# Two value loads cast on the way, key sums as products of their own, the ninth query chunk apart, W2 in five parts: a fused attention and feed-forward kernel on one core

## The chip, the core and the metric

The kernel runs on one core of one Trainium2 chip. The metric is device microseconds for one execution; lower is better. TensorE (PE), VectorE (DVE), ScalarE (ACT), GpSimd (POOL) and SyncE (SP) run side by side and wait for each other by semaphores. SP and GpSimd each issue DMA transfers on a queue of their own; in the profile SP's is the hardware queue q1 and GpSimd's the software queue q0.

## The reference

```
q_s = softmax of q over its 64 columns          # q, k, v: 8 batches x 8 heads x 576 x 64
k_s = softmax of k over the 576 rows
kv  = einsum('bhsd,bhse->bhde', k_s, v)         # 64 x 64 for each head
x   = einsum('bhsd,bhde->bhse', q_s, kv)        # laid out as 4608 tokens x 512
h   = x @ w_in                                  # 512 x 2048
g   = where(h > 0, h, exp(min(h, 0)) - 1)
out = g @ w_out                                 # 2048 x 512
```

## The kernel before, in words

The attention is done in sixteen **units**, each half the heads of one batch: unit n belongs to batch n // 2. A unit has 576 rows, cut into 9 **chunks** of 64. The feed-forward part works on nine **blocks** of 512 tokens. Block 0 takes the first 8 chunks of batch 0, which are units 0 and 1; the ninth chunk of each belongs to block 1.

For a unit, ACT takes the exponential of q (tile `QR`) and of k (`KR`, written as bfloat16 into the tile's own first half). DVE sums the rows of q (`ZQ`) and takes reciprocals (`RZQ`); DVE and POOL multiply (`QS`, float16). PE turns `QS` through the identity matrix `ID`, and a copy brings the result from PSUM (`PS`) to `qsT`. The value tile `VR` is cast to bfloat16 in `VB`, whose 65th column holds ones, so that one set of 36 small products (`kv_mm`, 64x65 each) gives the key-value matrix in 64 columns and the key sums in the 65th. `m` takes the reciprocals of those sums (`RZK`) and writes the scaled matrix to `MBLK`. A product of `MBLK` and `qsT` (`ao_parts`, `ao_mm`) gives x, which is copied to `XT`.

For a block, `hg_mm` multiplies `XT` by `W1` in eight groups of two tiles; `hg` applies the activation on ACT and DVE into `GR`; `out_mm` multiplies `GR` by `W2`. From block 2 on the second product is done in seven instead of eight quarter products (`pair`, L806). In block 0 the first three groups go part by part over the four slices kc of `W1`: slices 0 and 1 need `XT` of unit 0, slices 2 and 3 that of unit 1.

Even units use the buffers numbered 0 and odd units those numbered 1. Before the first product of block 0, PE multiplies the identity by itself (L892) where the plan sees it idle.

The order of the instructions on each engine is written out in the table `ORDER`: operations are numbered as the program creates them, and each engine's row lists the numbers. So a wait holds up everything behind it on its engine. Semaphore waits come from the tiles that each operation reads and writes.

At the start SP loads q of units 0 and 1, k and v of unit 0, k and v of unit 1, 576 KB each. GpSimd's queue loads the weights, and its first weight load waits for k of unit 0 (`gate`). Units 2 and 3 and `W2` (four parts of 1 MB) follow on GpSimd's queue.

Of the kernel before, what the change touches and what calls it, by code (L numbers as in the profile page):

```python
# [17 lines left out]
CH = 9  # L18
# [31 lines left out]
    "act": (  # L50
# [12 lines left out]
    "dve": (  # L63
# [37 lines left out]
}  # L101

AFTER = ((208, 196), (227, 255), (234, 268), (300, 281))


class Op:
    __slots__ = ("eng", "dur", "emit", "deps", "key", "idx", "start", "end",
                 "dma", "sem", "val", "clock", "nbytes", "side", "early", "alts")

# [157 lines left out]
def t_dve(n, fast=1):  # L267
    return n / 0.96 / fast + 74


def t_f32r(n):
    return (n + 32) / 2.4

# [816 lines left out]
```

## Time and profile before

| | |
|---|---|
| median of 3 runs | 292.26 us (292.03 to 292.69) |
| span of the profiled execution | 290.4 us, first to last instruction |
| median less span | 1.9 us; the page gives no total of its own for the profiled execution, so a span is turned into a time by adding this |
| PE busy | 280.6 us of the span (97%) |
| DVE, ACT, POOL busy | 225.5, 209.7, 167.8 us |
| first product of block 0 starts | 14.20 us |
| last product ends | 287.06 us |
| DMA | 36.70 MB read, 9.44 MB written |

The page gives busy times and shares, 40 slices of the span, the chain of work that ended last, and the costliest groups. A row of the timeline is: start, duration, engine, line, operation, tile written and read, count, and in brackets the idle time before it and what ended it. L277 is a copy helper, so its rows are told apart by their tiles.

### The profile page before, as it was taken

The numbers are of one execution on the slowest core, as the hardware profiler recorded it, in microseconds if no ns is written. First come the engines' busy times: TensorE is split into PE (matmuls) and PEld (weight loads), VectorE is DVE, ScalarE is ACT, GpSimd is POOL, SyncE is SP. The second block draws the span as 40 slices with busy tenths as digits, with TensorE's granted clock in tenths as the row PEclk, the third lists the DMA queues.
The fourth block names the chain that finished last, engine by engine and source line by source line (L and its number), as shares of the span: only waits on it lengthen the run. The fifth ranks groups of instructions, "written<-read, shape, count | busy, mean of one in ns | idle before, by whom it ended". The sixth has DMA issues, their size and how long they took to land.

```text
span 290.4 us, 5465 instructions
## 1 busy us (share of the span) xinstructions
PE 280.6 (97%) x2176; PEld 243.7 (84%) x2176; DVE 225.5 (78%) x425; ACT 209.7 (72%) x237; POOL 167.8 (58%) x161
## 2 busy tenths in 40 slices
PE   2899999999999999999999999999999999999995
PEld 0488787778888899989999988989999999988995
DVE  3758834777699978989996987688977786794884
ACT  4857839989899899968995598975385656665510
POOL 1991335523869778676574886757314234277741
PEclk9999999999999999999999999999999999999999
DMA  7999999798896838739939295313102002300334
GB/s 259 399 363 390 389 389 339 163 260 323 238 349 163 241 91 228 202 78 305 178 96 222 56 292 129 76 40 71 46 18 56 0 2 67 78 2 1 92 73 128
DMA packets 36474, 50.04 MB, mean 172 GB/s; under 512 B 16352, under 2 KB 18144, under 8 KB 36448
## 3 DMA queue, kind: packets, MB, share of 16 engines
q1 hardware_dynamic: 29680, 33.96, 43.7%
q0 software_dynamic: 6528, 15.47, 17.8%
q8 instruction: 17, 0.28, 0.5%
q10 hardware_dynamic: 240, 0.26, 0.3%
q14 instruction: 9, 0.07, 0.1%
HBM read 36.70 MB, written 9.44 MB: 159 GB/s over the span
## 4 chain that ended last, share of the span: by engine, by line
PE 94%; DMA 2%; POOL 2%; SPq 0%; issue 0%; DVE 0%
PE PS L620 46%; PE PS L806 32%; PE PS L673 10%; PE PS L538 3%; DMA KR<-in_k_dram 2%; PE PS L507 2%; POOL W L377 1%; POOL VB L277 0%; PE PS L457 0%; POOL QS L433 0%; SPq L359 0%; PE PS L550 0%; DVE OSB L815 0%
## 5 line engine op out<-in xcount | busy, mean ns | idle before, releaser
L620 PE MATMUL PS<-XT,W 128*128 128x512 f32 x576 | 142.0, 393 | 0.1
L620 PEld LDWEIGHTS PS<-XT,W 128*128 128x128 f32 x576 | 105.0, 188 | 21.2 <-DVE GR L659 0.5
L652 DVE SCALAR_TENSOR_TENSOR GR<-PS,GE 128x512 fp32r<-128x512 f32 x112 | 76.8, 686 | 18.7 <-ACT GE L648 16.7
L646 ACT ACTIVATE GE<-PS 128x1024 f32<-128x1024 f32 x56 | 57.4, 1025 | 40.0 <-PE PS L620 34.2
L757 POOL TENSOR_TENSOR GR<-GR 128x256 fp32r<-128x256 f32 (+1 forms) x48 | 47.2, 996 | 31.5 <-DVE SB L757 16.6
L648 ACT ACTIVATE GE<-GE 128x1024 f32<-128x1024 f32 x56 | 59.4, 1061 | 1.4
L806 PE MATMUL PS<-W,GR 128*128 128x256 f32 x336 | 53.7, 283 | 0.0
L806 PE MATMUL PS<-TB,GR 128*128 128x256 f32 x336 | 51.3, 283 | 0.0
L806 PEld LDWEIGHTS PS<-W,GR 128*128 128x128 f32 x336 | 47.6, 191 | 1.7
L806 PEld LDWEIGHTS PS<-TB,GR 128*128 128x128 f32 x336 | 45.7, 191 | 0.7
L433 POOL TENSOR_TENSOR QS<-QR,RZQ 128x1152 f16<-128x1152 f32 (+1 forms) x16 | 30.4, 1898 | 21.4 <-DVE RZQ L423 19.7
L815 DVE TENSOR_TENSOR OSB<-OSB,PS 128x256 f32<-128x256 f32 x84 | 34.7, 416 | 10.3 <-PE PS L806 9.2
L673 PE MATMUL PS<-W,GR 128*128 128x512 f32 x128 | 32.7, 396 | 0.0
L757 POOL TENSOR_TENSOR GR<-SB,GR 128x256 fp32r<-128x256 f32 (+1 forms) x18 | 17.3, 971 | 24.6 <-PE PS L806 12.7
L673 PEld LDWEIGHTS PS<-W,GR 128*128 128x128 f32 x128 | 23.3, 188 | 5.0 <-DMA W<-in_moe_w_out_dram 0.5
L757 POOL TENSOR_TENSOR SB<-GR 128x256 fp32r<-128x256 f32 (+1 forms) x20 | 19.2, 965 | 13.7 <-DVE GR L652 6.4
L421 DVE TENSOR_REDUCE ZQ<-QR 128x18 f32<-128x1152 f32 (+2 forms) x18 | 21.7, 1207 | 6.1 <-ACT QR L419 4.8
L757 DVE TENSOR_TENSOR GR<-GR 128x256 fp32r<-128x256 f32 (+1 forms) x36 | 21.3, 603 | 0.6 <-PE PS L806 0.6
L277 POOL CAST VB<-VR 128x1152 bf16<-128x1152 f32 (+1 forms) x11 | 11.9, 1084 | 13.1 <-DMA VR<-in_v_dram 13.1
L646 ACT ACTIVATE ESB<-PS 128x1024 f32<-128x1024 f32 x16 | 16.1, 1024 | 4.5 <-PE PS L620 3.4
L399 ACT ACTIVATE KR<-KR 128x1152 bf16<-128x1152 f32 x16 | 18.4, 1155 | 0.8 <-DMA KR<-in_k_dram 0.8
L277 ACT ACTIVATE XT<-PS 128x512 fp32r<-128x512 f32 (+6 forms) x23 | 13.6, 595 | 6.3 <-PE PS L538 3.2
(58 smaller groups left out, 271.4 us busy)
## 6 DMA issues: line engine op xcount, KB each, us to landing
out_dram<-OSB SPq DMA_DIRECT2D x61, 128.0 KB, 2.4
QR<-in_q_dram SPq DMA_DIRECT2D x12, 576.0 KB, 4.9
KR<-in_k_dram SPq DMA_DIRECT2D x12, 576.0 KB, 6.3
VR<-in_v_dram SPq DMA_DIRECT2D x12, 576.0 KB, 5.1
W<-in_moe_w_out_dram POOLq DMA_DIRECT2D x4, 1024.0 KB, 16.7
QR<-in_q_dram POOLq DMA_DIRECT2D x4, 576.0 KB, 12.1
VR<-in_v_dram POOLq DMA_DIRECT2D x4, 576.0 KB, 13.0
KR<-in_k_dram POOLq DMA_DIRECT2D x4, 576.0 KB, 11.1
```

The lines of the kernel that those rows point to most:

```text
L277: return e.activation(dst, src, AF.Copy) if e is self.nc.scalar else e.tensor_copy(dst, src)
L399: S.add("act", t_act(1152, False), lambda e: e.activation(ek[:, :, :, :].rearrange("p h c d -> p (h c d)"), flat(k), AF.Exp), key - 2, X=[ ...
L421: S.add("dve", t_dve(m), lambda e, qp=qp, zp=zp: e.tensor_reduce(zp, qp, AX.X, ALU.add), key - 3, R=[f"qR{i}{x}" for x in xs], W=[f"ZQ{i}{ ...
L433: lambda e, qp=q[:, :, a:b, :], rz=rz, dst=qs[:, :, a:b, :]: e.tensor_tensor(dst, qp, rz, ALU.mult),
L620: last = e.matmul(P[:, t * 512:(t + 1) * 512], self.W1[:, kc, tt * 128:(tt + 1) * 128], self.XT[:, kc, rc:rc + BLK], start=(kc == 0), stop ...
L646: S.add("act", t_act(1024, True), lambda e: e.activation(ge, P, AF.Exp), key, W=own, X=banks)
L648: S.add("act", t_act(1024, False), lambda e: e.activation(ge, ge, AF.Relu, bias=1.0, scale=-1.0), key, X=own)
L652: S.add("dve", t_dve(512 if j else 1024), lambda e, u=u: e.scalar_tensor_tensor(*(x[:, :, u, :] if j else x for x in (gt, P)), 0.0, ge[:, ...
L673: last = e.matmul(dst, self.tile(jb, jj, ts), self.W2[:, jj, c0:c1], start=(jj == 0), stop=(jj == 15))
L757: lambda e: e.tensor_tensor(dst, a, b, op), key, R=R, W=W, X=X, after=after)
L806: last = e.matmul(dst, a[i][:, y_, :], b[i][:, y_, :], start=start and i == 0 and y_ == 0, stop=stop and i == len(grps) - 1 and y_ == z - ...
L815: S.add("dve", t_dve(256), lambda e: e.tensor_tensor(dst, a, b, ALU.add), key, R=R, W=W, X=X, after=after)
```

## The change

- `load`: v of units 0 and 1 is loaded as bfloat16, into the first half of its own raw tile (`vp`). The casts to `VB` of these two units go. The two loads move from SP's queue to GpSimd's, and k of unit 1 with them. SP now issues three loads at the start: q of units 0 and 1, k of unit 0. v of unit 0 waits, in GpSimd's row, for q of unit 0 to land; the old `gate` of the first weight load goes.
- `key_sums`, `kv_plain`: for units 0 and 1 the 65th column is a set of 36 products of its own (64x1) with its own reciprocal, ahead of the 36 products of k and v (64x64).
- `stage_q`, `parts`, `rest`: the ninth query chunk of units 0 and 1 is staged, turned and multiplied apart, during block 0. Units 2 and 3 are cut into 7 and 2 chunks, and so are their loads of q.
- `load_w2`: `W2` comes in parts of 4, 4, 4, 2 and 2 tiles of 16; k and v of unit 3 stand ahead of the last two. The first product's last quarter in block 0 is cut in two accordingly.
- The exponentials of block 0 go to `GE` rather than to two `ESB` buffers; four `ESB` buffers serve the first half of block 1.
- `ORDER` is written anew for all engines.

The core of the diff:

```diff
-    def load(self, n, t, key, eng="gp"):
+    def load(self, n, t, key, eng="gp", c0=0, c1=CH, after=()):
...
+        if t == "v" and n in self.PLAIN:
+            dst = self.vp(n)[:, :, :, :].rearrange("p h c d -> p h (c d)")
...
+    PLAIN = (0, 1)
...
+    def key_sums(self, n, ps, key):
...
+                        last = e.matmul(P[hs, x:x + 1], ek[fs, h, c, :], VB[fs, h, c, D:D + 1],
+                                        start=(c == 0), stop=(c == CH - 1))
+            return last
+        S.add("pe", 400, mm, key, R=[f"kR{i}", f"VBone{vb}"], X=banks, side=1)
...
+        S.add("dve", 82, lambda e: e.reciprocal(rz[:, :].unsqueeze(2), PZ), key,
+              W=[f"RZK{i}"], X=banks)
...
+    def kv_plain(self, n, ps):
...
+                        last = e.matmul(P[hs, x:x + D], ek[fs, h, c, :], v[fs, h, c, :],
+                                        start=(c == 0), stop=(c == CH - 1))
...
-        for n, t in ((0, "q"), (1, "q"), (0, "k"), (0, "v"), (1, "k"), (1, "v")):
+        for n, t in ((0, "q"), (1, "q"), (0, "k")):
             self.load(n, t, -40, "sp")
-            if (n, t) == (0, "k"):
-                gate = S.ops[-1]
-        self.load_w1(0, 3, (0,), -30, [gate])
+        self.load(0, "v", -40, after=S.ops[-3:-2])
+        self.load(1, "k", -40)
+        self.load_w1(0, 3, (0,), -30)
+        self.load(1, "v", -40)
...
-        for g0, g1 in ((3, 4), (4, 5), (5, 6), (6, 8)):
+        for g0, g1 in ((3, 4), (4, 6), (6, 8)):
...
-        self.stage1(0, -8, vconv=CAST0)
+        self.stage1(0, -8)
         self.tp(0, AB, -9, TP0)
-        self.side(C, -6, self.kv_mm(0, C))
-        self.stage1(1, -5, vconv=CAST1)
+        self.key_sums(0, C, -7)
+        self.side(C, -6, self.kv_plain(0, C))
+        self.stage1(1, -5)
...
-        self.load(2, "q", -28)
-        self.load_w2(0, -29)
-        self.load_w2(1, -29)
-        for n, t in ((2, "k"), (2, "v"), (3, "q")):
+        self.load(2, "q", -28, c1=7)
+        self.load_w2(0, 4, -29)
+        self.load_w2(4, 8, -29)
+        for n, t in ((2, "k"), (2, "v")):
             self.load(n, t, -28)
-        self.load_w2(2, -27)
-        self.load_w2(3, -25)
+        self.load(3, "q", -28, c1=7)
+        self.load_w2(8, 12, -27)
         for t in "kv":
             self.load(3, t, -26)
+        for jj in (12, 14):
+            self.load_w2(jj, jj + 2, -25)
...
     "sp": (
-        "8 9 10 11 12 13 204 206 183 180 187 189 186 209 228 190 218 219 235 229 301 302 184 238 "
+        "8 9 10 230 232 209 206 213 215 212 235 254 216 244 245 261 255 327 328 210 264 375 207 "
```

How the table moves the instructions is seen in three places at the start. On ACT, before, from the first exponential of q to the copy of x (the brackets name the semaphores waited for: `D_` a load, by tile and issuing queue, `S_` an engine):

```order
L419 ACTIVATE QR0<-QR0 128x2x256 [waits D_qR0sp]
L419 ACTIVATE QR0<-QR0 128x2x320
L419 ACTIVATE QR1<-QR1 128x2x320 [waits D_qR1sp]
L399 ACTIVATE KR0<-KR0 128x1152 [waits D_kR0sp]
L277 ACTIVATE qsT0<-PS3 128x512 [waits S_pe]
L277 ACTIVATE VB0<-VR0 128x2x5x64 [waits D_vR0sp]
L419 ACTIVATE QR1<-QR1 128x2x256
L277 ACTIVATE qsT1_55<-PS1 128x640 [waits S_pe]
L277 ACTIVATE qsT0<-PS3 128x640 [waits S_pe]
L399 ACTIVATE KR1<-KR1 128x1152 [waits D_kR1sp]
L277 ACTIVATE VB1<-VR1_56 128x2x5x64 [waits D_vR1sp]
L277 ACTIVATE XT<-PS2 128x512 [waits S_pe]
```

The same stretch of ACT now:

```order
L431 ACTIVATE QR0<-QR0 128x2x256 [waits D_qR0sp0]
L431 ACTIVATE QR0<-QR0 128x2x256
L431 ACTIVATE QR1<-QR1 128x2x256 [waits D_qR1sp0]
L431 ACTIVATE QR1<-QR1 128x2x256
L412 ACTIVATE KR1<-KR1 128x1152 [waits D_kR1gp0]
L431 ACTIVATE QR0<-QR0 128x2x64
L412 ACTIVATE KR0<-KR0 128x1152 [waits D_kR0sp0]
L431 ACTIVATE QR1<-QR1 128x2x64
L282 ACTIVATE qsT0<-PS3 128x512 [waits S_pe]
L282 ACTIVATE qsT0<-PS3 128x512
L282 ACTIVATE XT<-PS2 128x512 [waits S_pe] x2
```

The two casts are gone, and the exponential of unit 1's keys, loaded by GpSimd's queue, now stands ahead of that of unit 0's keys, loaded by SP; both copies of unit 0's x are ACT's.

On POOL, before, from the first scaling of q to the second cast:

```order
L433 TENSOR_TENSOR QS0<-QR0,RZQ0 128x2x4x64 [waits S_dve]
L377 DMA W1<-in_moe_w_in_dram 128x1x768 [waits D_kR0sp]
L377 DMA W1<-in_moe_w_in_dram 128x1x768
L277 CAST VB0<-VR0 128x2x4x64 [waits D_vR0sp]
L377 DMA W1<-in_moe_w_in_dram 128x1x768 x2
L377 DMA W1<-in_moe_w_in_dram 128x4x256
L433 TENSOR_TENSOR QS1_54<-QR1,RZQ1 128x2x4x64 [waits S_dve]
L277 CAST VB1<-VR1_56 128x2x4x64 [waits D_vR1sp]
```

The same stretch of POOL now, from the identity matrix on:

```order
L343 AFFINE_SELECT ID<-ID 128x128
L367 DMA KR1<-in_k_dram 128x2x576
L367 DMA VR0<-in_v_dram 128x2x576 [waits D_qR0sp0]
L390 DMA W1<-in_moe_w_in_dram 128x1x768
L367 DMA VR1_56<-in_v_dram 128x2x576
L444 TENSOR_TENSOR QS0<-QR0,RZQ0 128x2x4x64 [waits S_dve]
L390 DMA W1<-in_moe_w_in_dram 128x1x768 x2
L444 TENSOR_TENSOR QS1_54<-QR1,RZQ1 128x2x4x64 [waits S_dve]
L367 DMA QR0<-in_q_dram 128x2x448 [waits S_gp]
L390 DMA W1<-in_moe_w_in_dram 128x1x768
```

Three loads of units 0 and 1 now stand on this engine, the first slice of `W1` between the two value loads, and 7 chunks of unit 2's q ahead of the last slice.

On PE, before, from the products of unit 0's keys and values to the first products with `W1`:

```order
L507 MATMUL PS2<-VB0,KR0 64x65 x35
L892 MATMUL PS0<-ID 128x512 [waits S_act]
L892 MATMUL PS0<-ID 128x512 x3
L550 MATMUL PS2<-qsT0,MBLK0 128x512 [waits S_act,S_dve]
L550 MATMUL PS2<-qsT0,MBLK0 128x512
L457 MATMUL PS1<-ID,QS1_54 128x128 [waits S_gp]
L457 MATMUL PS1<-ID,QS1_54 128x128 x3
L507 MATMUL PS0<-VB1,KR1 64x65 [waits S_act,S_gp]
L507 MATMUL PS0<-VB1,KR1 64x65 x35
L620 MATMUL PS2<-XT,W1 128x512 [waits D_w100,S_dve,S_act]
```

PE now, from unit 0's key sums to the first product with `W1`:

```order
L526 MATMUL PS2<-VB0,KR0 64x1 x35
L470 MATMUL PS3<-ID,QS0 128x128 [waits S_dve]
L470 MATMUL PS3<-ID,QS0 128x128 x3
L543 MATMUL PS2<-VR0,KR0 64x64 [waits D_vR0gp0,S_dve]
L543 MATMUL PS2<-VR0,KR0 64x64 x35
L470 MATMUL PS1<-ID,QS1_54 128x128 x4
L470 MATMUL PS1<-ID,QS1_54 128x128 [waits S_gp]
L470 MATMUL PS1<-ID,QS1_54 128x128 x3
L602 MATMUL PS2<-qsT0,MBLK0 128x512 [waits S_act,S_dve]
L602 MATMUL PS2<-qsT0,MBLK0 128x512
L543 MATMUL PS0<-VR1_56,KR1 64x64 [waits D_vR1gp0,S_dve]
L672 MATMUL PS3<-XT,W1 128x512 [waits D_w100,S_act]
```

Unit 0's products now wait for its key sums, which wait for its exponential; the dummy products of the identity all stand ahead of unit 1's key sums, eight in a row, and none after. Unit 1's products still stand right ahead of the first product with `W1`. They also wait for DVE, which reads unit 1's key sums out of the same bank; in DVE's row that reciprocal stands behind unit 0's `MBLK` and one cast of `qsT1`.

More of the change, by code (lines that the diff above doesn't have):

```diff
@@ L268, in t_dve, with cs @@
     return n / 0.96 / fast + 74
+def cs(name, c0=0, c1=CH):
+    return [f"{name}.{c}" for c in range(c0, c1)]
 def t_f32r(n):
@@ L380, in load_w1, with load_w2 @@
             dma=f"w1{g0}{kcs[0]}", nbytes=len(kcs) * (g1 - g0) << 17, after=after)
-    def load_w2(self, s, key, after=()):
+    def load_w2(self, jj0, jj1, key):
         w = self.w_out.rearrange("(jj p) c -> p jj c", p=128)
-        sl = slice(s * 4, (s + 1) * 4)
+        sl = slice(jj0, jj1)
         self.S.add("gp", ISSUE["gp"], lambda e: e.dma_start(self.W2[:, sl, :], w[:, sl, :]), key,
-                   W=[f"W2_{s}"], dma=f"w2{s}", nbytes=1 << 20, after=after)
+                   W=[f"W2_{s}" for s in range(jj0 // 2, jj1 // 2)], dma=f"w2{jj0}", nbytes=jj1 - jj0 << 18)
     def stage1(self, n, key, vconv="gp", what="qk"):
@@ L393, in stage1 @@
         flat = lambda t: t[:, :, :, :].rearrange("p h c d -> p (h c d)")
-        if "q" in what and n not in self.HALVED:
+        if "q" in what and n > 3:
             S.add("act", t_act(1152, False), lambda e: e.activation(flat(q), flat(q), AF.Exp),
-                  key - 3, X=[f"qR{i}0", f"qR{i}1"])
+                  key - 3, X=cs(f"qR{i}"))
         if "k" in what:
@@ L411, in stage1 @@
-        if "q" not in what:
-            return
-        qs = self.QS[self.alt(n)][:, :, :].rearrange("p c (h d) -> p h c d", h=2)
-        for c0, c1, xs in ([(c0, c1, [x]) for x, (c0, c1) in enumerate(self.HALF)]
-                           if n in self.HALVED else [(0, CH, [0, 1])]):
-            part, m = slice(c0, c1), (c1 - c0) * 128
-            qp, zp, rp = q[:, :, part, :], self.ZQ[i][:, :, part], self.RZQ[i][:, :, part]
-            if n in self.HALVED:
+            if n not in self.PLAIN:
+                dst, src = VB[:, :, :, 0:D], v[:, :, :, :]
+                cost = {"act": t_act(1152, False), "gp": 77 + 976}
+                S.add(dict(sorted(cost.items(), reverse=vconv == "gp")), None,
+                      lambda e: self.copy(e, dst, src), key - 50, R=[vname], W=[f"VB{vb}"])
@@ L419, in stage1, with stage_q @@
+        if "q" in what:
+            self.stage_q(n, key, self.parts(n)[:-1] if n < 4 else self.parts(n))
+    def stage_q(self, n, key, parts):
+        S, i, t = self.S, n % 2, self.alt(n)
+        q = self.RAW[i]["q"]
+        qs = self.QS[t][:, :, :].rearrange("p c (h d) -> p h c d", h=2)
+        for c0, c1 in parts:
+            m = (c1 - c0) * 128
+            qp, zp, rp = q[:, :, c0:c1, :], self.ZQ[i][:, :, c0:c1], self.RZQ[i][:, :, c0:c1]
+            if n < 4:
                 S.add("act", t_act(m, False), lambda e, qp=qp: e.activation(qp, qp, AF.Exp),
-                      key - 3, X=[f"qR{i}{x}" for x in xs])
+                      key - 3, X=cs(f"qR{i}", c0, c1))
@@ L426, in stage1 @@
-            for a, b, ys in cuts:
+                  key - 3, R=cs(f"ZQ{i}", c0, c1), W=cs(f"RZQ{i}", c0, c1))
+            for a, b in ((0, 4), (4, 7)) if (n in (2, 3) and c0 == 0) else ((c0, c1),):
                 m = (b - a) * 128
                 cost = {"gp": m * 2.0 + 30, "dve": t_dve(m)}
-                if n in self.BYPOOL and ys == [0]:
+                if n < 4 and a == 0:
                     cost = {"dve": t_dve(m), "gp": m * 2.0 + 30}
@@ L441, in ek, with tp @@
             "p (h c d) -> p h c d", h=2, c=CH)
-    def tp(self, n, ps, key, engs=("act", "act"), after=()):
+    def tp(self, n, ps, key, engs=("act", "act"), rest=False):
         S = self.S
@@ L515, in m @@
         PV = self.PS[ps][:, :].rearrange("p (f x) -> p f x", f=2)[:, :, at:at + D + 1]
-        S.add("dve", 82, lambda e: e.reciprocal(rz[:, :].unsqueeze(2), PV[:, :, D:D + 1]), key,
-              W=[f"RZK{i}"], X=banks)
+        if n not in self.PLAIN:
+            S.add("dve", 82, lambda e: e.reciprocal(rz[:, :].unsqueeze(2), PV[:, :, D:D + 1]), key,
+                  W=[f"RZK{i}"], X=banks)
         for h in range(2):
@@ L525, in part @@
     def part(self, n, x):
-        cut = 8 if n < 2 else self.split(n // 2)
+        cut = self.parts(n)[-1][0] if n < 4 else self.split(n // 2)
         return (0, cut) if x == (cut < 5) else (cut, CH)
@@ L552, in ao_parts @@
                 start=True, stop=True), key,
-                R=[f"qsT{self.alt(n)}{y}" for y in (0, 1)] + [f"MBLK{i}{y}" for y in ("", 0, 1)],
+                R=cs(f"qsT{self.alt(n)}", c0, c1) + [f"MBLK{i}{y}" for y in ("", 0, 1)],
                 X=[f"b{2 * ps + f}"], side=1)
@@ L633, in hg @@
         gw = sum((self.gnames(j, tp, (g,)) for tp in range(2)), [])
-        if j == 1:
-            gw += sorted(set(sum((self.early(u) for u in us), [])))
+        lent = [n for u in us for n in self.early(u)] if j == 1 else []
+        users = [o for n in sorted(set(lent)) for o in S.w.get(n, []) + S.r.get(n, [])]
         gt, ge = [x[:, us[0]:us[1] + 1:us[1] - us[0], :, :] for x in (self.GR, self.GE)]
@@ L639, in hg @@
         P = P[:, :].rearrange("p (c u t) -> p c u t", c=2, u=2) if j else P[:, :]
-        own = gw
-        if j < 2:
-            i = self.eslot % 2
-            self.eslot += 1
-            own = [f"E{i}"]
-            ge = self.ESB[i][:, :].rearrange("p (c u t) -> p c u t", c=2, u=2) if j else self.ESB[i][:, :]
-        S.add("act", t_act(1024, True), lambda e: e.activation(ge, P, AF.Exp), key, W=own, X=banks)
+        own, apart = gw, j == 1 and g < 4
+        if apart:
+            own = [f"E{g}"]
+            ge = self.ESB[g][:, :].rearrange("p (c u t) -> p c u t", c=2, u=2)
+        S.add("act", t_act(1024, True), lambda e: e.activation(ge, P, AF.Exp), key, W=own, X=banks, after=users)
         if how == "a":
@@ L650, in hg @@
             for u in range(2) if j else (slice(0, 2),):
-                mine = self.gnames(j, u, (g,)) + sorted(set(self.early(us[u]) if j == 1 else [])) if j else gw
+                mine = self.gnames(j, u, (g,)) if j else gw
                 S.add("dve", t_dve(512 if j else 1024), lambda e, u=u: e.scalar_tensor_tensor(
                     *(x[:, :, u, :] if j else x for x in (gt, P)), 0.0, ge[:, :, u, :] if j else ge,
-                    ALU.max, ALU.subtract), key, R=own if j < 2 else [], W=mine if j < 2 else [],
-                    X=banks + (mine if j > 1 else []))
+                    ALU.max, ALU.subtract), key, R=own if apart else [], W=mine if apart else [],
+                    X=banks + ([] if apart else mine))
         else:
@@ L659, in hg @@
             S.add("dve", t_dve(1024), lambda e: e.tensor_tensor(
-                gt, ge, P, ALU.max), key, R=own, W=gw, X=banks)
+                gt, ge, P, ALU.max), key, R=own if apart else [], W=gw if apart else [],
+                X=banks + ([] if apart else gw))
     def tile(self, j, jj, ts):
@@ L718, in w2 @@
         z0, z1 = GROUPS[grp]
-        return [f"W2_{s}" for s in range(z0 // 2, (z1 + 1) // 2)]
+        return [f"W2_{s}" for s in range(z0, z1)]
     def combos(self, key, grp):
@@ L786, in pair @@
             if (j, ts) == (WHOLE, 1):
-                over = ["qR10", "qR11"]
+                over = cs("qR1")
         else:
@@ L954, in loads, with rest, go, rests @@
             return 0, go
-        steps = [[first(2)], [wide(2), kv(2), loads(("q", 4), ("k", 4))],
-                 [first(3), loads(("v", 4)), ao(2, 0)], [ao(2, 1), wide(3)],
-                 [kv(3), loads(("q", 5), ("k", 5)), ao(3, 0)], [ao(3, 1)]]
+        def rest(n):
+            def go():
+                self.stage_q(n, key, self.parts(n)[-1:])
+                self.tp(n, AB, key, ("act",), rest=True)
+            return n, go
+        def rests():
+            def go():
+                self.side(AB, key, self.ao_mm(2, 1, AB), self.ao_mm(3, 1, AB, 128))
+                self.xt(2, 1, AB, key)
+                self.xt(3, 1, AB, key, at=128)
+            return 2, go
+        steps = [[first(2)], [wide(2), kv(2), loads(("k", 4))],
+                 [first(3), loads(("v", 4)), ao(2, 0)], [wide(3)],
+                 [kv(3), loads(("k", 5)), ao(3, 0)],
+                 [rest(2), loads(("q", 4)), rest(3), loads(("q", 5)), rests()]]
         def batch(b):
@@ L991, in program @@
             if g == 4:
+                for n in (0, 1):
+                    rest(n)[1]()
+                for n in (2, 3):
+                    self.load(n, "q", -24, c0=7)
                 self.side(AB, key, self.ao_mm(0, 1, AB), self.ao_mm(1, 1, AB, 64))
@@ L999, in program @@
             for ts in range(4):
-                self.out_mm(0, ts, (ts + 2) % 4, 4 * jq, 4 * jq + 4, key)
+                for jj in range(4 * jq, 4 * jq + 4, 2 if jq == 3 else 4):
+                    self.out_mm(0, ts, (ts + 2) % 4, jj, jj + (2 if jq == 3 else 4), key)
             key += 1
```

106 lines of the change are left out of this document (61 added, 45 removed), and 137 rows, old and new, of the table ORDER.

## The prediction

> **What bounds the kernel now.** I read the page first, for the engine that is never idle.
>
> ```profile
> span 290.4 us, 5465 instructions
> PE 280.6 (97%) x2176; PEld 243.7 (84%) x2176; DVE 225.5 (78%) x425; ACT 209.7 (72%) x237; POOL 167.8 (58%) x161
> PE   2899999999999999999999999999999999999995
> PE 94%; DMA 2%; POOL 2%; SPq 0%; issue 0%; DVE 0%
> ```
>
> PE is full from the third slice to the last, and 94% of the chain that ended last is PE. So I next asked what PE waits for in the whole run, and then for the chain in order of time (start, duration, what).
>
> ```profile
> PE PS L892 <- ACT QR L419: 5.5, 1, 5.5
> PE PS L550 <- DVE MBLK L520: 0.5, 1, 0.5
> PE PS L507 <- POOL VB L277: 0.2, 1, 0.2
> PE PS L457 <- POOL QS L433: 0.2, 1, 0.2
> ...
> 13.18 0.57 POOL VB L277
> 13.79 0.49 PE PS L507 x35
> 14.27 1.59 PE PS L620 x6
> ...
> 271.45 15.60 PE PS L806 x130
> 287.06 0.02 issue
> ```
>
> These four waits are all there are, and all fall before 13.8 us. From the first product with W1 on, PE runs without a gap until 287.06 us. Hence the time is the start of that stream, plus its length, plus a fixed end. The change can win only ahead of the start; it can lose there or by a new wait inside the stream.
>
> What sets the start is read from the timeline of the first 17 us (start, duration, engine, line, operation).
>
> ```profile
> 4.82 1.26 ACT L419 ACTIVATE QR<-QR 128x512 f32<-128x512 f32 x2 [2.59 <-DMA QR<-in_q_dram]
> 6.34 0.74 ACT L419 ACTIVATE QR<-QR 128x640 f32<-128x640 f32 x1 [0.26 <-DMA QR<-in_q_dram]
> 7.86 1.16 ACT L399 ACTIVATE KR<-KR 128x1152 bf16<-128x1152 f32 x1 [0.78 <-DMA KR<-in_k_dram]
> 13.00 0.73 POOL L277 CAST VB<-VR 128x512 bf16<-128x512 f32 x1
> 13.23 0.40 PE L457 MATMUL PS<-ID,QS 128*128 128x128 f16 x4 [0.15 <-POOL QS L433]
> 13.40 0.60 ACT L277 ACTIVATE XT<-PS 128x512 fp32r<-128x512 f32 x1
> 13.73 0.68 DVE L277 CAST qsT<-PS 128x512 fp32r<-128x512 f16 x1
> 13.79 0.49 PE L507 MATMUL PS<-VB,KR 64*64 64x65 bf16 x36 [0.16 <-POOL VB L277]
> 14.20 1.66 PE L620 MATMUL PS<-XT,W 128*128 128x512 f32 x6
> 14.33 0.17 DVE L516 RECIPROCAL RZK<-PS 128x2 f32<-128x2 f32 x1
> 14.53 0.61 DVE L520 TENSOR_TENSOR MBLK<-PS,RZK 64x128 fp32r<-64x128 f32 x2
> 15.70 0.62 PE L550 MATMUL PS<-qsT,MBLK 128*128 128x512 f32 x2
> 16.12 0.60 ACT L277 ACTIVATE XT<-PS 128x512 fp32r<-128x512 f32 x1 [2.12 <-PE PS L550]
> 16.16 13.32 PE L620 MATMUL PS<-XT,W 128*128 128x512 f32 x58
> ```
>
> The stream starts at 14.20. Right ahead of it stand unit 1's keys and values (13.79), which waited for the cast on POOL (13.00 to 13.73). That cast and its partner on ACT are what the change takes away.
>
> **The change part by part.** Removed first: the four casts. The value load of unit 1 landed 8.8 us after its issue at 3.58, at 12.4, and its products began 1.4 us later; so if all else stood still, at most 1.4 us could be won. But the loads move too, and here the sum is decided. The rows of single transfers (count, issue duration, issue time; then issue to landing):
>
> ```profile
> L359 SPq DMA_DIRECT2D KR<-in_k_dram x1: 470/470/470, 1.8 to 1.8; - x1
> DMA to landing us min/median/max: 6.1/6.1/6.1
> L359 SPq DMA_DIRECT2D VR<-in_v_dram x1: 515/515/515, 3.6 to 3.6; - x1
> DMA to landing us min/median/max: 8.8/8.8/8.8
> L377 POOL DMA_DIRECT2D W<-in_moe_w_in_dram x1: 714/714/714, 8.1 to 8.1; - x1
> DMA to landing us min/median/max: 5.2/5.2/5.2
> W<-in_moe_w_in_dram POOLq DMA_DIRECT2D x4, 384.0 KB, 5.3
> L359 POOL DMA_DIRECT2D VR<-in_v_dram x1: 724/724/724, 50.6 to 50.6; - x1
> DMA to landing us min/median/max: 4.2/4.2/4.2
> 1.58 0.29 POOL L338 TENSOR_SCALAR_AFFINE_SELECT ID<-ID 128x128 f16<-128x128 f16 x1 [1.14 <-DVE ID L337]
> ```
>
> SP's loads stand in line at 1.5 us each: k of unit 0 lands at 1.75 + 6.1 = 7.85, v of unit 1, three loads on, at 12.4, and (12.4 - 7.85) / 3 = 1.52. GpSimd's queue is no slower by itself: the value load issued at 50.6 landed in 4.2 us. But the first W1 load, smaller by a third and issued at 8.14, took 5.2 and landed at 13.3, after all of SP's, while those kept their 1.5 us. So a GpSimd load issued behind SP loads got nothing until they were done.
>
> By that, k of unit 1, issued at 1.87 (end of the identity) behind SP's three, lands one load after k of unit 0: 7.85 + 1.5 = 9.35. Before it landed two loads after, but nothing of unit 0 waited for it. Now ACT's order does: unit 1's exponential stands ahead of unit 0's. Step by step:
>
> - ACT: the four exponentials of q are done by 7.6 (6.34 + 2 x 0.63, by the row at 4.82). ACT then waits for unit 1's keys: 9.35 + 1.16 = 10.53. One chunk of q follows, 128 wide; the nearest row is a 128-wide copy, 276 ns:
>
> ```profile
> L277 ACT ACTIVATE XT<-PS 128x128 fp32r<-128x128 f32 x2 | 0.6, 276 | 0.0
> ```
>
> It ends at 10.8, and unit 0's exponential at 11.97. Its keys have lain there since 7.85; before, it ended at 9.02.
> - PE: unit 0's key sums start at 12.05. No row shows 64x1 products. Above, I bound them by the 64x65 set, which holds PE for 0.41 us (13.79 to 14.20); below, by a quarter of that, 0.1, were width all. I take 0.41, as 36 weight loads remain either way: 12.46. Four turns of q follow, 0.40 by the row at 13.23: 12.86. Then the keys and values of unit 0; the values are there (third in GpSimd's line, 9.35 + 1.5 = 10.9).
> - DVE: from the start of that set to the reading engine's start are 0.54 us (13.79 to 14.33), then `MBLK` 0.61: 14.01. The reciprocal, now earlier, is hidden by the four turns.
> - PE: unit 0's x at 14.07 (0.06 as from POOL's 13.73 to 13.79). ACT's copy follows at 14.49 (0.42, as from 15.70 to 16.12) and ends at 15.09.
> - DVE: after `MBLK`, cast of `qsT` 0.68 and the reciprocal of unit 1's sums 0.17: 14.86. Only then may unit 1's products begin, at 14.92; v of unit 1 has been there since 13.4 (10.9, plus 1.0 for the W1 slice between, plus 1.5). They hold PE for 0.41.
> - Start of the stream: 15.33, where it was 14.20. Loss 1.13.
>
> In the stream: two turns of single chunks that were ahead of it, 0.1 each at the row's 0.40 for four: +0.2, bounded below by nothing if they fill a wait. All else there is the same work in other pieces, beside PE: the small exponentials, reductions and copies of the ninth chunks lie on ACT and DVE, which are idle for 28% and 22% of the span. If that cover is gone, PE waits for a copy of 0.3 us once or twice; I keep 0.3 for the range. W1's last early slice stands behind 448 KB of q and lands at 13.4 + 1.0 + 1.0 + 1.2 + 1.0 = 17.6; PE reaches it after 14 products and two of x at 0.23 (58 in 13.32), at 19.0. W2 in five parts is called in the same order with a later stream, so it costs nothing. v of unit 0 waits on POOL for q of unit 0 (4.8), and behind it stand a W1 load, v of unit 1 and the first scaling of q; three issues of 0.71 end at 7.0, and PE does not turn what that scaling makes before 10.6. That wait is free.
>
> Sum: 1.13 + 0.2 = 1.3. Span 290.4 + 1.3 = 291.7. The median stood 1.9 above the span, so 293.6 us.
>
> The cast on the way is in no row I can name for certain. If such a load moves like any other of 576 KB, it takes 1.5 us; if it is paced by what it writes, 0.75; if casting halves the rate, 3. I take 1.5, the row of the same source bytes. The shorter price changes nothing above, since v waits for nobody there.
>
> **The rivals.**
>
> *GpSimd's load goes first* (not slower). Unit 1's keys are issued at 1.87, unit 0's at 1.75: nearly together, with q of unit 1 still in line. If the line were kept so that unit 1's keys went first, they would land at 7.85 and unit 0's at 9.35. ACT would end unit 0's exponential at 9.35 + 1.16 = 10.51 instead of 11.97, and all steps behind it come 1.47 earlier (v of unit 1, 13.4, then just makes it): 293.6 - 1.5 = 292.1. With values paced by what they write, key sums at 0.1 and turns at half their price (0.3, 0.2 and, in the stream, 0.2 less), 291.4. It decides from a landing of unit 1's keys before 8.0. Against it: the W1 load that stood back. For it: that row had SP's loads issued long before it.
>
> *PE at half pace* (slower still). The dummy products show PE slow at first:
>
> ```profile
> 5.51 2.32 PE L892 MATMUL PS<-ID 128*128 128x512 f16 x5 [5.51 <-ACT QR L419]
> 10.82 1.04 PE L892 MATMUL PS<-ID 128*128 128x512 f16 x4
> ```
>
> Five took 464 ns each, the later four 260. Between, PE was kept at work almost without a gap. Now eight stand in a row, 5.5 to 9.2, and then PE idles until 10.6, and again until 12.05. If the fast pace needs an unbroken run of 4 to 5 us, as from 5.5 to about 10 here, it comes at 16.2 to 17.4 when counted from 12.05; stream products from 15.33 on would cost half as much again to twice, 0.4 to 1.0, and the small products ahead about 0.3: 294.6, to 295.4 if the count begins anew at 14.07. The Trainium skill, TensorE: Matmul & The Clock Gate, Part 1, says that PE runs at half clock until it has been busy for one window of about 3.4 us, and that the window's place is free from run to run; the two rows agree with a change of pace, and by that rule eight products in a row may or may not suffice.
>
> *The cast halves the rate* (slower). Then v of unit 0 lands at 12.35 and v of unit 1 at 16.3; its products at 16.4 and the stream at 16.8: 295.1.
>
> *The change does nothing*: excluded, since the start of the stream is rebuilt as a whole.
>
> **How the numbers follow.** About 0.2% (0.6 us) is what a measurement can tell from no change. Chances: forecast 0.44, half pace 0.24, halved cast rate 0.07, GpSimd first 0.25. Of the last I count 0.12 beyond 0.6 us faster, 0.12 within; of the forecast, 0.02 falls within if the turns and key sums cost least. The forecast's own range is 292.9 to 294.1: the turns and key sums at their least, or one wait and a copy more. The range reaches from 291.9, inside GpSimd first, to 295.3, which leaves out the faster half of that rival and the upper end of the slow ones.
>
> **What would show it.** Right: unit 1's exponential of k starts near 9.4 and unit 0's ends near 12.0 on ACT; the first product with W1 starts near 15.3; PE's waits still end before it. Wrong at the first step: unit 1's keys land before unit 0's. Wrong at the size: 64x1 products that take far from 0.41 us, or a product with W1 that takes over 0.3 us after the start. Wrong altogether: new PE waits after 20 us, above all on W2 or on the copies of the ninth chunks.

## The result, and the profile after

The changed kernel takes 294.46 us (median of 4 runs, 293.97 to 295.25); the kernel before took 292.19 us beside it (292.03 to 292.69). The ratio is 1.0079, 95% interval 1.0063 to 1.0095: slower by 2.3 us. The profiled execution of the changed kernel is its fastest run, 293.97 us with a span of 292.1 us, so 1.9 us lie around the span as before; the other three runs have spans of 292.4, 292.9 and 293.4. Their mean granted clocks are 0.994 (the profiled run), 0.994, 1.000 and 0.988; e7 below comes back to that.

The page's head and its rows of PE and of the granted clock:

```profile
span 292.1 us, 5610 instructions
PE 281.7 (96%) x2244; PEld 244.6 (84%) x2244; DVE 232.0 (79%) x438; ACT 204.7 (70%) x233; POOL 174.5 (60%) x172
PE   2799999999999999999999999999999999999995
PEclk9889999999999999999999999999999999999999
```

PE is as full as before, and the loss is again in the first three slices. The clock row is new: slices two and three show 8, where the row of before shows 9 throughout. What PE waited for in the whole span (microseconds in all, times, longest):

```profile
PE PS L945 <- ACT QR L431: 5.4, 1, 5.4
PE PS L526 <- ACT KR L412: 1.9, 2, 1.4
```

PE waits for unit 1's exponential of k (1.4) and for unit 0's (0.5), and for nothing from the start of the stream to the end. The timeline of that stretch:

```profile
9.15 1.16 ACT L412 ACTIVATE KR<-KR 128x1152 bf16<-128x1152 f32 x1 [1.81 <-DMA KR<-in_k_dram]
10.42 1.15 ACT L412 ACTIVATE KR<-KR 128x1152 bf16<-128x1152 f32 x1
11.62 0.45 PE L526 MATMUL PS<-VB,KR 64*64 64x1 bf16 x36 [0.47 <-ACT KR L412]
12.00 0.23 PEld L470 LDWEIGHTS PS<-ID,QS 128*128 128x128 f16 x4
12.36 0.48 PE L543 MATMUL PS<-VR,KR 64*64 64x64 bf16 x36
12.91 0.61 DVE L572 TENSOR_TENSOR MBLK<-PS,RZK 64x128 fp32r<-64x128 f32 x2 [0.60 <-PE PS L543]
13.67 1.19 PE L602 MATMUL PS<-qsT,MBLK 128*128 128x512 f32 x2
14.79 0.69 PE L543 MATMUL PS<-VR,KR 64*64 64x64 bf16 x36
15.41 2.02 PE L672 MATMUL PS<-XT,W 128*128 128x512 f32 x6
```

Unit 1's exponential stands ahead of unit 0's (9.15, 10.42), and the stream starts at 15.41 instead of 14.20. Two rows have grown without a change of shape: unit 0's two products for x took 1.19, and the first six products with W1 took 2.02 instead of 1.66. Before, unit 0's x was this row:

```profile
12.35 0.73 PE L550 MATMUL PS<-qsT,MBLK 128*128 128x512 f32 x2 [0.49 <-DVE MBLK L520]
```

The same stretch by windows of 3.4 us (length, PE busy, instructions, granted clock, share and GB/s of the DMA engines), now and, in the last line, the first window of the kernel before:

```profile
9.40:12.80 3.40, 1.96 (x117) 1.00 1.19 289
12.80:16.20 3.40, 3.40 (x55) 0.50 1.10 359
16.20:19.60 3.40, 3.40 (x17) 1.00 1.36 392
...
9.40:12.80 3.40, 2.91 (x52) 1.00 1.13 399
```

After a window in which PE was busy for 1.96 of 3.40 us, the next one ran at half the clock, and the stream's first products fell into it. In the kernel before, PE was busy for 2.91 us of the first window, and the clock stayed full.

From the single products in the two traces: the stream starts 1.21 us later, its 25th product 1.61 later (20.24 and 21.85), the last product 1.86 later (286.76 and 288.62). So of these 1.86 us, 1.21 lie ahead of the stream, 0.40 in its first 24 products, and 0.25 in all the rest. The work behind the last product is 0.15 shorter, which leaves the 1.7 us by which the span has grown.

### The profile page after: what moved, and what is told of

Read it like the earlier page. It is cut to its first block, busy times and chain, and to the rows that moved or that the text cites. A ratio compares the mean times of both kernels' runs of the same rounds, so it can differ in the third digit from the quotient of the medians.

```text
span 292.1 us, 5610 instructions
## 1 busy us (share of the span) xinstructions
PE 281.7 (96%) x2244; PEld 244.6 (84%) x2244; DVE 232.0 (79%) x438; ACT 204.7 (70%) x233; POOL 174.5 (60%) x172
## 3 DMA queue, kind: packets, MB, share of 16 engines
HBM read 36.70 MB, written 9.44 MB: 158 GB/s over the span
## 4 chain that ended last, share of the span: by engine, by line
PE 95%; DMA 2%; ACT 1%; DVE 0%; issue 0%; POOL 0%; POOLq 0%
PE PS L672 46%; PE PS L857 32%; PE PS L724 10%; PE PS L590 3%; DMA KR<-in_k_dram 2%; PE PS L558 2%; PE PS L470 1%; ACT KR L412 1%; PE PS L602 1%; PE PS L543 0%; PE PS L526 0%; DVE OSB L866 0%; POOL ID L343 0%; DVE MBLK L354 0%; ACT QR L431 0%
## 5 line engine op out<-in xcount | busy, mean ns | idle before, releaser
L672 PE MATMUL PS<-XT,W 128*128 128x512 f32 x576 | 143.6, 394 | 0.0
L702 DVE SCALAR_TENSOR_TENSOR GR<-PS,GE 128x512 fp32r<-128x512 f32 (+1 forms) x120 | 84.5, 705 | 23.4 <-ACT GE L698 21.4
L696 ACT ACTIVATE GE<-PS 128x1024 f32<-128x1024 f32 x68 | 69.4, 1025 | 46.1 <-PE PS L672 40.1
L698 ACT ACTIVATE GE<-GE 128x1024 f32<-128x1024 f32 x62 | 65.8, 1061 | 1.7
L857 PEld LDWEIGHTS PS<-W,GR 128*128 128x128 f32 x336 | 47.6, 191 | 1.6
L444 POOL TENSOR_TENSOR QS<-QR,RZQ 128x1152 f16<-128x1152 f32 (+4 forms) x19 | 31.5, 1657 | 17.2 <-DVE RZQ L435 17.0
L808 POOL TENSOR_TENSOR SB<-GR 128x256 fp32r<-128x256 f32 (+1 forms) x24 | 23.9, 1001 | 14.8 <-DVE GR L702 7.4
L808 POOL TENSOR_TENSOR GR<-SB,GR 128x256 fp32r<-128x256 f32 (+1 forms) x18 | 17.4, 974 | 23.1 <-PE PS L857 12.7
L433 DVE TENSOR_REDUCE ZQ<-QR 128x18 f32<-128x1152 f32 (+4 forms) x22 | 22.2, 1017 | 4.6 <-ACT QR L431 3.7
L282 ACT ACTIVATE OSB<-PS 128x256 f32<-128x256 f32 (+1 forms) x23 | 9.0, 406 | 14.1 <-PE PS L857 13.6
L282 POOL CAST VB<-VR 128x1152 bf16<-128x1152 f32 x9 | 10.4, 1153 | 10.4 <-DMA VR<-in_v_dram 9.4
L282 ACT ACTIVATE XT<-PS 128x512 fp32r<-128x512 f32 (+6 forms) x20 | 12.4, 627 | 5.6 <-PE PS L590 3.6
```

The costliest lines, as they stand in the source:

```text
L282: return e.activation(dst, src, AF.Copy) if e is self.nc.scalar else e.tensor_copy(dst, src)
L433: S.add("dve", t_dve(m), lambda e, qp=qp, zp=zp: e.tensor_reduce(zp, qp, AX.X, ALU.add), key - 3, R=cs(f"qR{i}", c0, c1), W=cs(f"ZQ{i}", c ...
L444: lambda e, qp=q[:, :, a:b, :], rz=rz, dst=qs[:, :, a:b, :]: e.tensor_tensor(dst, qp, rz, ALU.mult),
L672: last = e.matmul(P[:, t * 512:(t + 1) * 512], self.W1[:, kc, tt * 128:(tt + 1) * 128], self.XT[:, kc, rc:rc + BLK], start=(kc == 0), stop ...
L696: S.add("act", t_act(1024, True), lambda e: e.activation(ge, P, AF.Exp), key, W=own, X=banks, after=users)
L698: S.add("act", t_act(1024, False), lambda e: e.activation(ge, ge, AF.Relu, bias=1.0, scale=-1.0), key, X=own)
```

## The experiments

The theory was three causes in a row: unit 0's chain stands behind unit 1's late keys; the idle time that this makes costs the clock; the stream has some 0.25 us more work. The fourth experiment showed another, hidden behind these. All times are medians beside the kernel before on the same chip (292.01 to 292.18 us). "Start" is that of the first product with W1; "24 products" the time from it to the 25th; both are of the one profiled run, which for e1 and e5 was the slowest, while the time is the median of all.

| kernel | us | ratio (95%) | start | 24 products |
|---|---|---|---|---|
| before | 292.19 | 1 | 14.20 | 6.04 |
| after | 294.46 | 1.0079 (1.0063 to 1.0095) | 15.41 | 6.44 |
| e1: order of the keys | 294.55 | 1.0073 (1.0058 to 1.0088) | 15.64 | 6.75 |
| e2: dummies | 293.72 | 1.0051 (1.0039 to 1.0063) | 14.91 | 6.59 |
| e3: both | 293.77 | 1.0055 (1.0043 to 1.0067) | 14.37 | 7.01 |
| e4: k of unit 1 on SP | 293.5 | 1.0043 (1.0031 to 1.0055) | 13.91 | 7.46 |
| e5: e4, W1 first | 292.57 | 1.0023 (1.0010 to 1.0036) | 14.19 | 6.07 |
| e6: e2, W1 first | 293.2 | 1.0032 (1.0020 to 1.0045) | 14.89 | 6.05 |
| e7: after, W1 first | 294.63 | 1.0086 (1.0073 to 1.0100) | 16.07 | 7.04 |
| e8: e5, unit 4 later | 294.68 | 1.0089 (1.0075 to 1.0102) | 14.28 | 6.06 |
| e9: e8, key sums later | 294.87 | 1.0099 (1.0082 to 1.0117) | 13.85 | 6.80 |
| e5 again | 292.94 | 1.005 (1.001 to 1.009) | 14.09 | 6.03 |

**e1: unit 0's keys first.** The two exponentials of k and the products behind them change places; the dummy products, which a plan places, are set by a small table instead.

```diff
-ACT  42 38 37 105 21 111 ...    # 37: exp of unit 1's k, 21: of unit 0's
+ACT  42 38 21 105 37 111 ...
-PE   56 32 34 30 36 50 ...      # 56: key sums of unit 1, 34: of unit 0
+PE   32 34 30 36 56 50 ...
```

> Unit 0's exponential of k ahead of unit 1's on ACT, unit 0's key sums ahead of unit 1's on PE; loads and all else as in the changed kernel, eight dummy products. Theory A (the start is late because unit 0's chain stands behind a load that lands late): unit 0's exponential runs from about 9.5 (its keys landed at 9.4 in the changed kernel, the last engine late) to 10.6 instead of ending at 11.6, and the first product with W1 starts near 14.5 instead of 15.4: about 0.9 us faster than the changed kernel, 293.5. Theory B (the loss is PE's pace, not the start): the time stays within 0.3 us of the changed kernel's 294.5 whatever the start does.

Measured 294.55 us, nothing gained. PE now waits 1.5 us in one piece for the exponential of unit 0's keys, and all that follows ran slowly:

```profile
11.50 0.61 PE L474 MATMUL PS<-ID,QS 128*128 128x128 f16 x4
13.88 1.20 PE L606 MATMUL PS<-qsT,MBLK 128*128 128x512 f32 x2
15.64 2.33 PE L676 MATMUL PS<-XT,W 128*128 128x512 f32 x6
```

Four turns took 0.61 instead of 0.40, the products for x 1.20, the first six of the stream 2.33. Here the clock did not fall back, it had not come up: the key sums, at 10.93, were slow already (0.64 instead of 0.45), and the trace's first record of the granted clock starts at 17.11. The views count the time ahead of that record as 1.00, so in this run only the durations show the slow pace. The order alone could not be judged: PE's pace took what it may have won.

**e2: dummies that keep PE busy.** The changed kernel with eleven dummy products instead of eight ahead of unit 1's key sums, and two more ahead of unit 0's.

```diff
+SPARES = {56: 11, 34: 2}
+SPARE_PS = {34: 1}
```

> The changed kernel with eleven instead of eight dummy products at first, and two more ahead of unit 0's key sums; the start stays where it is. Theory B: PE's granted clock does not fall back after 12.8, the six first products take 1.7 instead of 2.0 us, the 24 first products end 0.4 us earlier, and the time is 0.4 to 0.8 us less than the changed kernel's with less spread from run to run. Theory A alone: no difference beyond 0.2 us, and the spread stays.

Measured 293.72 us, 0.7 less than the changed kernel, with runs within 0.5 us of each other instead of 1.3. The same windows as above:

```profile
9.40:12.80 3.40, 3.12 (x120) 1.00 1.18 271
12.80:16.20 3.40, 3.12 (x68) 1.00 1.12 373
```

PE busy for 3.12 us of the first window kept the full clock in the second; six products take 1.67 again, and the start moves from 15.41 to 14.91. That PE's clock is a cause is shown. But a new wait stands in the stream, 0.2 us for W1.

**e3: both.**

```diff
 ACT, PE: as e1
+SPARES = {32: 11, 56: 1}
```

> Both edits: unit 0's exponential first, eleven dummy products at first and one ahead of unit 1's key sums. If A and B both hold and add up: first product with W1 near 14.5 at full pace, 292.7 to 293.1. If only A: as the first edit alone. If only B: as the second alone.

Measured 293.77 us, no better than e2, although the stream starts at 14.37, 0.54 earlier. The waits of PE say where it went:

```profile
PE PS L949 <- ACT QR L435: 5.7, 1, 5.7
PE PS L676 <- DMA W<-in_moe_w_in_dram: 0.6, 1, 0.6
```

**e4: k of unit 1 on SP's queue again,** as SP's fourth load, with the two exponentials in the order in which the keys then come; the values stay on GpSimd's queue and are cast there. On that queue both values now go ahead of the first slice of W1, and on DVE one cast of `qsT` ahead of unit 0's `MBLK`.

```diff
-        self.load(1, "k", -40)
+        self.load(1, "k", -40, "sp")
-ACT  42 38 37 105 21 111 31 33 54 55
+ACT  42 38 21 105 111 31 33 37 54 55
-PE   56 32 34 30 36 50 48 52
+PE   32 34 30 50 48 36 56 52
+SPARES = {32: 8, 48: 3}
```

> Unit 1's keys loaded by SP again, as its fourth load; GpSimd's queue takes the two values and then the first slice of W1; unit 0's exponential first on ACT; on DVE one cast of qsT ahead of unit 0's MBLK and unit 1's key sum reciprocal before the other; three dummy products between the turns. Theory A: unit 0's keys land at 7.8 and its exponential ends at 9.0; the start is then set by unit 0's values (10.9) and unit 1's keys (9.4 to 10.8): first product with W1 near 13.5, 0.7 us ahead of the kernel before; time 291.6 to 292.2, as the work in the stream is 0.25 us longer. Rival: what was gained by the value loads is lost by mixing two queues, the keys on SP land later than 9.4 and the start is at 14.2 or later: 292.4 or more.

Measured 293.5 us, not 291.6 to 292.2. The first half came as expected, and better: the stream starts at 13.91, ahead of the kernel before. Then it stops at 18.97:

```profile
13.91 1.66 PE L677 MATMUL PS<-XT,W 128*128 128x512 f32 x6
...
18.97 3.95 PEld L677 LDWEIGHTS PS<-XT,W 128*128 128x128 f32 x18 [1.54 <-DMA W<-in_moe_w_in_dram]
18.97 7.21 PE L677 MATMUL PS<-XT,W 128*128 128x512 f32 x30 [1.11 <-DMA W<-in_moe_w_in_dram]
```

It waits for W1's last early slice, which landed at 18.93. In the kernel before that slice landed at 16.28. In the changed kernel the seven chunks of unit 2's query are issued ahead of it, and it lands at 18.90 as well; there the stream reaches it at 19.36, too late to notice. The next three runs test that.

**e5, e6 and e7: W1 ahead of unit 2's query,** made from e4, from e2 and from the changed kernel itself.

```diff
-POOL  41 65 17 18 19 20 66 108      # 65: load of unit 2's q, 17 to 20: W1, 66: W2
+POOL  41 17 18 19 20 66 65 108
-ACT   54 55 128 88 91 ... 123 124 134    # 128: exp of unit 2's q
+ACT   54 55 88 91 ... 123 124 128 134
 DVE   likewise with its sums (129, 130)
```

> As e4, but the rest of W1 is issued ahead of unit 2's seven query chunks, which then come behind the first part of W2, with their exponential and sums behind the third group of the hidden layer. Theory A (three costs lie one behind the other: the late chain, the clock, the order of W1 and unit 2's query): slice 3 of W1 lands by about 17.0 instead of 18.9, no product with W1 waits, the stream starts at 13.9 as in e4 and loses nothing at 18.97, so e4's 293.5 less its stalls of 1.27 and 0.26: about 292.0 (291.6 to 292.4), at or below the kernel before (292.1). Rival (the transfers as a whole are behind, not one slice): the wait only moves to a later slice of W1 or to W2, and the time stays at 293.0 to 293.6.

> As e2 (the changed kernel with dummies that keep the clock full), with the same order of W1 and unit 2's query as e5. Theory A: e2's waits for W1 (0.2 on the products, some 0.37 with the weight loads) go, so about 293.4 (293.1 to 293.6) against e2's 293.7: what is left above the kernel before is the late start alone (14.9 against 14.2) and the stream's own 0.2 to 0.3. Rival: no difference from e2 (293.7), the waits were slack.

> The changed kernel with only the order of W1 and unit 2's query changed, no dummies. Theory A: the stream starts at 15.4 and slice 3 of W1 is not waited for even where it lands at 18.9, so nothing is gained: 294.2 to 294.7 (the changed kernel: 294.5), with the changed kernel's spread, since TensorE's clock falls back as there. Rival (W1's late slices already cost the changed kernel something): 293.7 to 294.1.

e6 and e7 settle what the order of W1 is worth. Alone it changes nothing (294.63 against 294.46). With the clock kept it is worth 0.5 (293.2 against 293.72), and 24 products take 6.05 again. And dummies are worth 0.7 without it and 1.4 with it. The costs lie one behind the other: each is seen only once the one ahead of it is gone.

The profile of e7 (295.23, where its runs lie between 293.9 and 295.24) shows that the slow pace has two forms:

```profile
5.50 3.60 PE L946 MATMUL PS<-ID 128*128 128x512 f16 x8 [5.50 <-ACT QR L432]
10.51 0.64 PE L527 MATMUL PS<-VB,KR 64*64 64x1 bf16 x36 [1.41 <-ACT KR L413]
16.07 2.65 PE L673 MATMUL PS<-XT,W 128*128 128x512 f32 x6
```

As in e1, the key sums were slow already, and the stream's products came every 0.43 us until 18.3 and every 0.23 from then on. The trace's first record of the granted clock starts at 18.25 (at 9.40 in the changed kernel, at 9.02 in e6). So in e1 and e7 PE came up to full pace only inside the stream; in the changed kernel's profiled run it came up at 9.40, with the same eight dummies, and fell back from 12.81 to 16.22. Against e6, whose last product starts at 287.84, the run with the fall is 0.8 us later (288.62) and e7's is 2.0 later (289.81). The 1.4 us are a median over runs of both kinds. One fall of 3.4 us at half clock in a span of 292 makes a mean granted clock of 0.994, two make 0.988. In e1 the three runs with 0.994 took 293.5 to 294.5 and the three with 1.000, the profiled one among them, 294.7 to 295.3; a mean of 1.000 can so hide a late rise. What decides between the two forms was not tested.

e5 measured 292.57 us: the waits for W1 are gone, 24 products take 6.07, and the kernel is 0.2% above the kernel before, not at it. Seven of its twelve runs were 292.1 to 292.6, five 293.2 to 294.1. Its profile is of the slowest, 294.1:

```profile
PE PS L595 <- DVE qsT L287: 1.3, 1, 1.3
...
50.20 1.17 ACT L413 ACTIVATE QR<-QR 128x1152 f32<-128x1152 f32 x1 [2.54 <-DMA QR<-in_q_dram]
51.40 1.35 DVE L438 TENSOR_REDUCE ZQ<-QR 128x18 f32<-128x1152 f32 x1 [2.21 <-ACT QR L413]
53.38 0.66 PE L595 MATMUL PS<-qsT,MBLK 128*128 128x128 f32 x4 [1.25 <-DVE qsT L287]
```

Unit 4's query came late (50.2, and 47.9 in e6); its exponential and sums stand ahead of the copy of a ninth chunk on ACT and DVE, and PE waited for that copy.

**e8: unit 4's sums later.**

```diff
-ACT  224 275 276           # 224: exp of unit 4's q, 275, 276: hidden layer
+ACT  275 224 276
-DVE  185 227 228 192 214   # 227, 228: unit 4's sums, 185, 192: copies of last chunks
+DVE  185 192 214 227 228
```

> e5 with unit 4's exponential and its sums put behind the work that does not need that load (the exponential behind the next one of the hidden layer, the sums on VectorE behind the two copies of the last query chunks). e5's runs fell in two groups, 292.1 to 292.6 and 293.2 to 294.1, and its profile, one of the slowest, shows PE waiting 1.25 for such a copy, which stood behind a sum that waited for unit 4's query (landed 50.2). Theory A: the second group was this wait; it goes, the first group stays: 292.3 (292.0 to 292.5). Rival: the two groups come from the transfers themselves (one engine of the 16 late by 2 to 3 us), which then makes something else wait: again runs at 293 or more, median 292.5 to 293.2.

Measured 294.68 us, 2.1 more than e5: a miss. The wait for the copy is gone, but the exponential now splits two steps of the activation, the sums stand ahead of the next, and PE waits for what these make:

```profile
PE PS L729 <- DVE GR L714: 0.6, 1, 0.6
PE PS L677 <- DVE XT L287: 0.5, 1, 0.5
PE PS L677 <- DVE GR L707: 0.4, 1, 0.4
```

In this run unit 4's query had landed by 47.6, so the loss is that of the order itself. At that place ACT and DVE have no room for the 1.2 us of the exponential and the 1.6 us of the sums.

**e9: key sums of unit 1 behind unit 0's x,** and unit 1's keys and values behind the first two products with W1. On DVE the reciprocal of those sums goes one place back.

```diff
-PE   36 56 52 53 58 76 77   # 56: key sums, 52, 53: x of unit 0, 58: kv of unit 1
+PE   36 52 53 56 76 58 77
```

> e8 with unit 1's key sums behind the product of unit 0's query with its block (in e4 that product started 12.72, held by the key sums that waited for unit 1's exponential), and unit 1's keys and values behind the first two products with W1. Theory A: the stream starts at 13.55 instead of 13.9 to 14.2, bounded by the first slice of W1 (landed 13.3 to 13.6), and the time is 291.9 (291.6 to 292.2), below the kernel before (292.15). Rival: the first slices of W1 are late as well (13.6 and 14.8), the start moves by under 0.2, 292.2 to 292.4, no gain over e8.

Measured 294.87 us, e8's loss in it. The start did move, from 14.28 to 13.85, but the 25th product came 0.31 later than in e8 (20.65, 20.34). PE's waits at the start, of e8 and then of e9:

```profile
PE PS L531 <- ACT KR L417: 0.7, 1, 0.7
...
PE PS L607 <- DVE MBLK L577: 0.7, 1, 0.7
```

Unit 0's x waits for DVE's `MBLK` in any case: in e8 the key sums start (12.71) just as `MBLK` is done, so both orders leave PE idle for 0.7 there. What moved is the work behind. x starts 0.42 earlier (12.67 instead of 13.09) and the stream 0.43, but unit 1's keys and values now stand in the middle of it, and 24 products take 0.74 longer. The 36 small products take 0.4 of that; most of the rest is that the product with W1 on either side of them is slower (0.34 from start to start for the first one behind them, where the next take 0.23). Neither theory had that.

**A second look at e5.**

> The same kernel as e5, for a second profile, since the first was of the slowest of its twelve runs. If the wait of 1.25 for VectorE's copy (behind unit 4's late query) is what parts the two groups of e5's runs, a profile at 292.1 to 292.6 shows no such wait and unit 4's query landed on all 16 engines by about 48.5, and one at 293.2 or more shows it again. Rival: a profile of the lower group has the wait too, or one of the upper group hasn't.

Measured 292.94 us (7 runs, ratio 1.005, interval 1.001 to 1.009). The profile is of an upper run, 293.68, and has no wait for the copy. It has another:

```profile
PE PS L729 <- DMA W<-in_moe_w_out_dram: 0.7, 1, 0.7
PE PS L531 <- ACT KR L417: 0.6, 2, 0.4
```

So the rival holds: the upper runs have not one cause. No run of the lower group was profiled. In this run one DMA engine of the 16 finished the second part of W2 2.7 us behind the first (29.24 to 31.93); in the other, unit 4's query 3.0 us behind (47.15 to 50.17). No version beat the kernel before.

## Why the prediction was right, and where it was not

Slower was right, and 294.46 lies in the range. The forecast of 293.6 was 0.9 short, and its own range ended at 294.1; the whole range held because it also covered the rival of the slow pace.

- **Unit 1's keys late, unit 0 behind them** (the first step): right in the outcome, not in the whole reason. Keys landed at 9.13 (said 9.35), unit 0's exponential ended at 11.57 (11.97; the 10.53 on the way there should be 10.51). The GpSimd load did stand back: issued at 2.10, its first packet moved at 6.38. But "nothing until they were done" was too strong: from then on both queues moved packets (in the kernel before, W1's first packet moved at 11.22, and SP's last load landed at 12.34). And unit 0's keys landed late too, on 15 engines by 8.22 and on the last at 9.44, instead of lying there since 7.84. So unit 1's keys did land ahead of unit 0's, the forecast's own sign of a wrong first step. It changed little here because ACT's order puts them first anyway; but the transfers hold unit 0 back as well as the order on ACT, and e1's order alone could not bring it back to 9.02.
- **Key sums at 0.41, turns at 0.40:** 0.38 and 0.36. Width counts for next to nothing in these small products, as assumed.
- **The sum to the start, 15.33:** measured 15.41, but by two misses that cancel. With the clock kept full (e2) the same chain starts the stream at 14.91, so the chain cost 0.7 and not 1.13: unit 0's key sums start there at 11.71 and not at 12.05 (keys 0.2 earlier, and the small exponential overlaps the large ones), and the rest was 0.1 shorter. The slow clock put 0.5 on top.
- **PE at half pace** was a rival at 294.6 to 295.4, apart from the forecast. It came on top of the forecast's chain. In e1 and e7 it came as the rival has it: full pace at 17.11 and 18.25, where it said 16.2 to 17.4 (its own 4 to 5 us from 12.05 give 16.05 to 17.05). In the profiled run of the changed kernel it came otherwise: up at 9.40, down again at 12.81. By e6 and e7 it is worth 1.4 us in the median run. This is the step that failed: a cost that follows from the forecast's own gaps (PE idle from 9.2 to 10.6 and again to 12.05) belongs in its sum. 0.7 for the chain, 1.4 for the clock and 0.25 in the stream make 2.35; measured were 2.3. The Trainium skill, TensorE: Matmul & The Clock Gate, Part 1, lets the clock fall after at least one idle window of about 3.4 us; here it fell after a window with PE busy for 1.96 of 3.4 us, and stayed with 3.12. The measurement decides: PE need not be idle for the whole window. Nor does busy time alone tell. In e5 the clock stayed full after 2.48 of 3.41 us (9.14 to 12.55); in e7 3.35 of 3.42 us (11.42 to 14.84), most of them in products 128 wide or less, did not bring it up, while 2.98 of 3.41 us with the wide dummies (5.99 to 9.40) did in the changed kernel. What is counted stays open.
- **In the stream +0.2:** 0.25 from the 25th product on in the changed kernel, 0.38 in e6. Right, at the low side.
- **W1's last early slice at 17.6, needed at 19.0:** right that nothing waits, wrong by 1.3 on the landing (18.90): 15 of the 16 engines had delivered by 17.51, the last had not. The margin was not 1.4 but 0.5, and that only because the slow clock held the stream back to 19.36; at full clock (e2, e3) PE waits.
- **The cast on the way at 1.5 us:** the first value load landed 1.3 after unit 0's keys and 1.6 after unit 1's; so the transfer took the time of its source's bytes. *GpSimd's load goes first* and *the cast halves the rate* are both out.

## What to carry to other kernels

A change that takes work off the head of a pipeline also takes away what kept the matrix engine's clock up: price the gaps that it opens by the clock of the window that follows, in the sum and not as another case. Read the pace from the durations of known rows and not from the clock column alone, which reads 1.00 ahead of its first record. When several things are late, they hide one behind the other; an experiment that removes only the first shows the second, so remove them in pairs before saying that one is worth nothing. And a load moved forward is paid for by all that stands behind it in the queue: list when each of them is needed, and leave each a margin of some 2 to 3 us where one engine of the 16 can be that late.

## What the runs showed of the hardware

One packet of the instruction queue goes together with one DMA engine that stays behind for a long time. The queue's row in the windows from 14 to 17 us of the changed kernel:

```profile
q0 software_dynamic: 386, 1.05, 107.8%
q8 instruction: 1, 0.02, 2.1%
```

It is one packet of 16 KB, at 16.24, and took 0.99 us. The load that landed before it did so within 0.7 us on all 16 engines (15.87 to 16.53); the two behind it took 2.0 and 2.1 (16.86 to 18.90, 18.25 to 20.38). In e4 the packet came at 14.86, and the spread grew from 0.9 to 1.8 there; in e6 it came at 15.77, and the spread grew from 0.8 to 1.6. In the kernel before no such packet falls between 14 and 17 us; it came at 20.88, and its landings spread from 0.6 to 1.9 us only after that, when the early slices of W1 had landed. That the packet is the cause is read from the times in four traces; no run took it away. Why it comes earlier (the changed kernel has 145 instructions more) stays open too.
